# TensorE's order written out by hand in the attention stage: expert steps with attention pieces between them, and the first chunk's chain ahead of the second's

## The chip, the cores and the metric

The kernel runs on one core of one Trainium2 chip. The time is device microseconds for one execution of the whole program, the median of three runs. The engines are TensorE (PE; its weight loads are listed as PEld), VectorE (DVE), ScalarE (ACT), GpSimd (POOL) and SyncE (SP), which issues nearly all DMAs here. Each engine executes its instructions in the order in which they stand in the program.

## What is computed

Two parts, one behind the other. First a linear attention with complex, diagonal decay, over 4 batches, 8 heads, 768 positions and 48 dimensions; its output, as 3072 tokens of 384, is the input of a mixture of eight experts whose weights P are balanced over all tokens:

```python
# attention
scale = np.minimum(mag, 0.999) / (mag + 1e-06)      # mag = |a|
for t in range(S):
    S_re, S_im = ar * S_re - ai * S_im, ar * S_im + ai * S_re
    S_re = S_re + k[t] outer v[t]
    y[t] = q[t] @ S_re
# experts, x = y as (3072, 384)
P = np.exp(x @ w_gate - max)
for _ in range(8):
    P /= P.sum(1, keepdims=True) + 1e-09
    P /= P.sum(0, keepdims=True) + 1e-09
    P *= N / E
for e in range(E):                                   # w1: 384 x 1024, w2: 1024 x 384
    out += P[:, e:e + 1] * (np.maximum(x @ w1[e], 0.0) @ w2[e])
```

## The kernel before

The tokens are cut into 12 sub-chunks of 256, three for each batch, and each sub-chunk into two chunks of 128. Four kinds of work touch a sub-chunk i.

`elem(i)` (L262) is the elementwise part, on DVE and ACT. `chain` (L313) normalises the decays, forms their running products (a scan of complex products, `cmul`, L244 to 260), divides the keys by them (kh, L376) and multiplies the queries with them (z, L381). Both go to DRAM (kd, L377; qd, L382), since attention needs them with heads in another layout. For sub-chunk 0 the two chunks have a chain each; the later ones do both chunks in one.

`mix(i)` (L384) is the attention of the sub-chunk. It loads keys (ks, L397) and queries (qs, L398) back from DRAM into two buffers that the chunks use in turn; the last column of qs holds the chunk's total decay, which ACT copies into rr and rn (L400 to 402). For each chunk and each group of four heads PE transposes keys (ktp, L417; copied to kt on ACT, L419), forms the chunk's state contribution (U, L421) and the scores (sp, L424; DVE copies their lower triangle into sc, L427), and multiplies scores with values and queries with the state so far into the output (y, L438). Then DVE updates the state (L448 to 459). The output is x, split into a high and a low half (xh, L461; xl, L462) so that matmuls with the fast type keep float32 precision.

`logits(i)` (L466) makes the gate's logits of a sub-chunk. A `moe` step (L142) is 128 of one expert's 1024 hidden units for the 256 tokens: nine layer-1 matmuls (ph, L162 to 164), a relu that ACT writes twice (hh, L168; hf, L169), the difference on DVE (hl, L170), and six layer-2 matmuls (po, L152 to 154). Only experts 0 and 1 are computed in this way, 16 steps for each sub-chunk and 192 in all. Their weights are split into two halves by `load_w` (L124), with PE matmuls against the identity (wd, L136 and 137).

The program is written as mix(i), then the 16 steps of sub-chunk i-1, then elem(i+1), and a scheduler decides each engine's order in this part, from that order of writing and from a simulated timeline. The steps of the last two sub-chunks are written behind the first half of the balancing of P (check, L481; `sinkhorn`, L497; `rows` and `columns`, L514 to 528, of whose eight iterations four run here and where each column sum needs a PE matmul, L524). The last stage, experts 2 to 7 (from the first product P, L693), already has PE's order fixed by the order of writing.

Of the kernel before, what the change touches and what calls it, by code (L numbers as in the profile page):

```python
# [13 lines left out]
H, D = 8, 48  # L14
# [10 lines left out]
RING = 12  # L25
TR = 4
# [25 lines left out]
class Net:  # L52
# [9 lines left out]
    def build(self):  # L62
# [3 lines left out]
        with ExitStack() as ctx:  # L66
# [38 lines left out]
            with ExitStack() as c2:  # L105
                with ExitStack() as c1:
                    with ExitStack() as ca:
                        self.phase1(c1, ca)
                    self.phase2a(c2)
                    for u in range(2):  # L110
                        for i in range(ns - 2, ns):
                            self.moe1(i, (u,))
                        if u == 0:
                            self.raw_w()
                            self.prep_w()
                            self.prep_w()
                with tc.manual_schedule(engines={mybir.EngineType.PE}):
                    self.phase2b(c2)
# [5 lines left out]
    def load_w(self, e, f, pool, stage, tag):  # L124
        nc = self.nc
        t = pool.tile([128, 2, 2 * C], F32R, tag="w", name=f"w{e}_{f}")
        raw = stage.tile([128, 2 * C], F32, tag=tag, name=f"wr{e}_{f}")
        nc.sync.dma_start(raw, self.w[e, f])
        nc.scalar.activation(t[:, 0, :], raw, AF.Copy)
        for j in range(2):  # L130
            cs = slice(j * C, j * C + C)
            if j == 0:
                d = self.psA.tile([128, C], F32, tag="ph", name=f"wd{e}_{f}_{j}")
            else:
                d = self.psB.tile([128, C], F32, tag="po", name=f"wd{e}_{f}_{j}")
            nc.tensor.matmul(d, self.ident, raw[:, cs], start=True, stop=False)  # L136
            nc.tensor.matmul(d, self.nident, t[:, 0, cs], start=False, stop=True)
            nc.scalar.activation(t[:, 1, cs], d, AF.Copy)
        self.wt[e, f] = t

    def moe(self, e, fs, xs, T, done):
        nc = self.nc  # L142
        nt = T // 128
        po = [self.psB.tile([128, C], F32, tag="po", name=f"po{e}_{i}") for i in range(nt)]
        pend = []

        def l2(f, hh, hl, first, last):
            w2h = self.wt[e, f][:, 0, C:]
            w2l = self.wt[e, f][:, 1, C:]
            for i in range(nt):  # L150
                s = slice(i * 128, i * 128 + 128)
                nc.tensor.matmul(po[i], hh[:, s], w2h, start=first, stop=False)  # L152
                nc.tensor.matmul(po[i], hh[:, s], w2l, start=False, stop=False)  # L153
                nc.tensor.matmul(po[i], hl[:, s], w2h, start=False, stop=last)  # L154

        xh, xl = xs
        for j, f in enumerate(fs):
            w = self.wt[e, f]
            ph = self.psA.tile([128, T], F32, tag="ph", name=f"ph{e}_{f}")
# [5 lines left out]
            hh = self.hp.tile([128, T], F32R, tag="hh", name=f"hh{e}_{f}")  # L165
            hl = self.hp.tile([128, T], F32R, tag="hl", name=f"hl{e}_{f}")
            hf = self.hp.tile([128, T], F32, tag="hf", name=f"hf{e}_{f}", bufs=2)
# [3 lines left out]
            pend.append((f, hh, hl, j == 0, j == len(fs) - 1))  # L171
            if len(pend) > 1:
                l2(*pend.pop(0))
        l2(*pend.pop(0))
        for i in range(nt):
            done(i, po[i])

    def phase1(self, c1, ca):
# [31 lines left out]
        units = [(0, list(range(NF))), (1, list(range(N1)))]  # L210
        self.units = units
        self.elem(0, True)
        for f in range(NF):
            self.load_w(0, f, self.wp, wx, "w")
        for f in range(N1):
            if NF + f < RING:
                self.load_w(1, f, self.wp, wx, "w")
            else:
                self.load_w(1, f, wx, self.xp, "xh" if f % 2 else "xl")
        for i in range(ns):  # L220
            self.mix(i)
            if i == ns - 1:
                self.logits(i)
            if i > 0 and i + 1 < ns:
                self.moe1(i - 1)
            if i + 1 < ns:
                with ExitStack() as ctx:
                    if i == 0:
                        ctx.enter_context(tc.issue_after(self.gl.ins))
                    self.elem(i + 1)  # L230

    def moe1(self, i, us=(0, 1)):
        nc = self.nc
        for u in us:
            e, fs = self.units[u]

            def done(k, po, u=u, i=i):
                st = self.xp.tile([128, C], F32, tag="yst", name=f"yst{u}_{i}_{k}")
                nc.scalar.activation(st, po, AF.Copy)
                nc.sync.dma_start(self.ye_d[u][i * (SUB // 128) + k], st)  # L240

            self.moe(e, fs, self.xs[i], SUB, done)

    def cmul(self, L, R, n, alloc):  # L244
# [15 lines left out]
        V.tensor_tensor(R[:, 1], a[:, 1], b[:, 0], ALU.add)  # L260
# [51 lines left out]

    def chain(self, i, ns_, zt, qk, alloc):  # L313
# [25 lines left out]
        zr = z.rearrange("p a g (r b) -> p a g r b", r=TR)  # L339
        for r in range(1, TR):  # L340
            self.cmul(zr[:, :, :, r - 1], zr[:, :, :, r], TB, alloc)
        ze = zr[:, :, :, TR - 1]
        for r in range(1, TR):
            self.cmul(ze[:, :, :, r - 1::TR], ze[:, :, :, r::TR], TB // TR, alloc)
        d = 1
        while d < TB // TR:
            m = TB // TR - d
            self.cmul(ze[:, :, :, TR - 1:TR - 1 + TR * m:TR], ze[:, :, :, TR - 1 + TR * d::TR], m, alloc)
            d *= 2
        zs = ze.rearrange("p a g (c s) -> p a g c s", s=TR)  # L350
        m = TB // TR - 1
        sh = list(zs[:, :, :, 1:, :TR - 1].shape)
        self.cmul(zs[:, :, :, :m, TR - 1:].broadcast_to(sh), zs[:, :, :, 1:, :TR - 1], m * (TR - 1), alloc)
        for r in range(0, TR - 1, 2):
            R = zr[:, :, :, r:min(r + 2, TR - 1), 1:]
            L = ze[:, :, :, :TB - 1]
            if R.shape[3] == 1:
                self.cmul(L, zr[:, :, :, r, 1:], TB - 1, alloc)
            else:
                self.cmul(L.unsqueeze(3).broadcast_to(list(R.shape)), R, R.shape[3] * (TB - 1), alloc)  # L360
# [3 lines left out]
        nc.scalar.activation(sq, z, AF.Square)  # L364
# [10 lines left out]
        for a in range(2):  # L375
            V.tensor_tensor(kh[:, a], x, z[:, a], ALU.mult)  # L376
            nc.sync.dma_start(  # L377
                kd[a, :, ns_].rearrange("(c p) n t -> p c (n t)", c=NCT),
                kh[:, a].rearrange("p (c n) t -> p c (n t)", c=NCT))
        for a in range(2):  # L380
# [5 lines left out]
    def mix(self, i):  # L386
# [6 lines left out]
        for c in range(NCH):  # L393
# [15 lines left out]
            for g in range(2):  # L409
                hs = range(4 * g, 4 * g + 4)  # L410
                if not lastc:
                    if i == 0:
                        kt_p = self.psB.tile([128, 4, SK], F32, tag="po", name=f"ktp{i}_{c}_{g}")
                    else:
                        kt_p = self.psS.tile([128, 4, SK], F32, tag="s", name=f"ktp{i}_{c}_{g}")
                    for j, h in enumerate(hs):
                        nc.tensor.transpose(kt_p[:, j, :], ks[:, h, :], self.ident[:SK, :SK])  # L417
                    kt = tmp.tile([128, 4, SK], F32, tag="kt", name=f"kt{i}_{c}_{g}", bufs=2)
                    nc.scalar.activation(kt, kt_p, AF.Copy)  # L419
                    for j, h in enumerate(hs):  # L420
                        nc.tensor.matmul(U[:, h, :], kt[:, j, :], vt[:, c, slot(h):slot(h) + D], start=True, stop=True)  # L421
                sp = self.psS.tile([128, 4, CH], F32, tag="s", name=f"sp{i}_{c}_{g}")
                for j, h in enumerate(hs):
                    nc.tensor.matmul(sp[:, j, :], ks[:, h, :], qs[:, h, :CH], start=True, stop=True)  # L424
                ss = self.sc[self.isc]
                self.isc = 1 - self.isc
                nc.vector.copy_predicated(ss, self.mask, sp)  # L427
                for b in range(2):
                    for inter in range(1 if first else 2):
                        for j, h in enumerate(hs):  # L430
# [4 lines left out]
                            rw = qs[:, h, :CH] if inter else ss[:, j, :]  # L435
# [3 lines left out]
            if c == 0 and i > 0:  # L439
                self.logits(i - 1)  # L440
# [22 lines left out]
        for a, t in ((0, xh), (1, xl)):  # L463
            nc.sync.dma_start(self.x_d[i // NS][:, i % NS, a], t.bitcast(F32).rearrange("p c (j t) -> p c j t", t=CH))

    def logits(self, i):  # L466
# [7 lines left out]
        nc.scalar.activation(ls, lp, AF.Copy)  # L474
        lt = self.psS.tile([128, SUB // 128, E], F32, tag="s", name=f"lt{i}")
# [3 lines left out]
        nc.scalar.activation(self.P[:, i * n:(i + 1) * n, :], lt, AF.Copy)  # L479

    def check(self, sp):  # L481
# [9 lines left out]
        nc.vector.tensor_reduce(ok[:, 7:8], ok[:, 0:7], AX.X, ALU.min)  # L491
        tp = self.psK.tile([1, 128], F32, tag="po", name="okp")
# [4 lines left out]
    def sinkhorn(self, sp):  # L497
# [433 lines left out]
```

## Time and profile before

| | us |
|---|---|
| median of three runs | 1891.73 (1889.19 to 1897.45) |
| the profiled execution, own time | 1894.79 |
| its span in the profile | 1892.9 |
| PE busy in the span | 1794.9 (95%) |
| DVE busy | 1362.0 (72%) |
| ACT busy | 732.9 (39%) |
| first product P of the last stage | 717 |

The span is what the trace covers; the execution's own time has 1.9 us around it. The stages of the span are: start, with the weights of experts 0 and 1 and sub-chunk 0 (to 120 us); attention with the steps of sub-chunks 0 to 9 between (120 to about 652); the first half of the balancing with the last steps (652 to 717); experts 2 to 7 (717 to 1893).

### The profile page before, as it was taken

To read this page: it belongs to the slowest core of one execution; us is meant where nothing else is said; L and a number is where in the kernel's file an instruction comes from. 1 tells how busy PE (TensorE), PEld (TensorE's weight loads), DVE (VectorE), ACT (ScalarE), POOL (GpSimd) and SP (SyncE) were. 2 spreads that over 40 slices of the span, in tenths; PEclk is the share of its full clock that TensorE was granted. 3 is DMA by queue.
4 is the path that set the end of the run, shared out by engine and by line. 5 is a ranking of instruction groups with operands and counts; after the bars stand their busy time and mean duration, and the time that the engine had idled before them with its cause. 6 is when DMAs were issued, how large, how long until landed. Compare 5 with 4: busy or idle time off the path is not lost.

```text
span 1892.9 us, 30256 instructions
## 1 busy us (share of the span) xinstructions
PE 1794.9 (95%) x12012; PEld 1745.2 (92%) x12012; DVE 1362.0 (72%) x3060; ACT 732.9 (39%) x1610; POOL 6.4 (0%) x15
## 2 busy tenths in 40 slices
PE   5879988898999999999999999999999999999998
PEld 3779888888989999999999999999999999999998
DVE  7777778878877377876767676778786767676754
ACT  7434444444443353433333333334342424242421
POOL 1000000000000000000000000000000000000000
PEclk9888999999899999999999999999999999999999
DMA  6555555665454322220101010123130201010100
GB/s 199 128 136 120 145 146 138 146 146 128 136 127 117 118 92 68 84 84 17 51 17 51 18 51 17 51 92 125 51 101 1 67 1 57 11 51 17 51 22 31
DMA packets 137207, 151.84 MB, mean 80 GB/s; under 512 B 7264, under 2 KB 116576, under 8 KB 137056
## 3 DMA queue, kind: packets, MB, share of 16 engines
q1 hardware_dynamic: 136256, 149.42, 28.5%
q8 instruction: 96, 1.57, 0.3%
q14 instruction: 55, 0.45, 0.1%
q10 hardware_dynamic: 800, 0.39, 0.1%
HBM read 107.17 MB, written 42.61 MB: 79 GB/s over the span
## 4 chain that ended last, share of the span: by engine, by line
PE 73%; DMA 12%; DVE 10%; ACT 2%; issue 2%; SPq 1%; DVEq 0%; ACTq 0%
PE po L656 10%; PE po L654 10%; PE po L655 10%; PE P L693 9%; PE P L695 9%; PE P L694 9%; DMA qs<-qd 4%; DMA qd<-z 3%; PE po L152 2%; PE ph L162 2%; PE ph L163 2%; PE po L154 2%; PE po L153 2%; PE ph L164 2%; PE sp L424 2%
## 5 line engine op out<-in xcount | busy, mean ns | idle before, releaser
L656 PE MATMUL po<-wc,hl 128*128 128x384 f32 x1152 | 385.6, 335 | 1.9 <-DVE hl L715 1.8
L654 PE MATMUL po<-wc,hh 128*128 128x384 f32 x1152 | 385.2, 334 | 0.0
L655 PE MATMUL po<-wc,hh 128*128 128x384 f32 x1152 | 385.2, 334 | 0.0
L714 ACT ACTIVATE hh<-c 128x384 fp32r<-128x384 f32 x384 | 201.1, 524 | 319.5 <-DVE c L703 318.0
L715 DVE SCALAR_TENSOR_TENSOR hl<-c,hh 128x384 fp32r<-128x384 f32 x384 | 212.2, 553 | 66.6 <-ACT hh L714 58.6
L656 PEld LDWEIGHTS po<-wc,hl 128*128 128x128 f32 x1152 | 216.5, 188 | 2.9 <-DVE hl L715 2.9
L655 PEld LDWEIGHTS po<-wc,hh 128*128 128x128 f32 x1152 | 216.5, 188 | 0.0
L654 PEld LDWEIGHTS po<-wc,hh 128*128 128x128 f32 x1152 | 216.5, 188 | 0.0
L708 ACT ACTIVATE s<-P 128x384 f32<-128x384 f32 x192 | 94.2, 491 | 276.7 <-PE P L695 276.4
L162 PE MATMUL ph<-xh,w 128*128 128x256 f32 x576 | 166.2, 289 | 7.7 <-ACT hf L169 5.8
L163 PE MATMUL ph<-xl,w 128*128 128x256 f32 x576 | 166.2, 289 | 4.8 <-DVE xl L462 4.8
L164 PE MATMUL ph<-xh,w 128*128 128x256 f32 x576 | 165.3, 287 | 0.0
L693 PE MATMUL P<-B,wa 128*128 128x384 f32 x480 | 160.7, 335 | 1.4 <-DVE c L703 1.4
L695 PE MATMUL P<-B,wa 128*128 128x384 f32 x480 | 160.5, 334 | 0.0
L694 PE MATMUL P<-B,wa 128*128 128x384 f32 x480 | 160.5, 334 | 0.0
L170 DVE TENSOR_TENSOR hl<-hf,hh 128x256 fp32r<-128x256 f32 x192 | 79.5, 419 | 100.1 <-ACT hf L169 96.6
L152 PE MATMUL po<-w,hh 128*128 128x384 f32 x384 | 137.0, 357 | 1.3 <-ACT hh L168 1.3
L153 PE MATMUL po<-w,hh 128*128 128x384 f32 x384 | 132.0, 344 | 0.0
L703 DVE TENSOR_TENSOR c<-P,u 128x384 f32<-128x384 f32 x192 | 106.4, 554 | 31.4 <-PE P L695 29.8
L168 ACT ACTIVATE hh<-ph 128x256 fp32r<-128x256 f32 x192 | 73.0, 380 | 142.5 <-PE ph L164 135.8
L703 DVE TENSOR_TENSOR u<-u,s 128x384 f32<-128x384 f32 x96 | 53.4, 556 | 100.2 <-ACT s L708 99.9
L162 PEld LDWEIGHTS ph<-xh,w 128*128 128x128 f32 x576 | 111.7, 194 | 9.4 <-ACT hf L169 6.3
(182 smaller groups left out, 3686.0 us busy)
## 6 DMA issues: line engine op xcount, KB each, us to landing
raw<-in_w_dram SPq DMA_DIRECT2D x48, 768.0 KB, 4.3
qs<-qd SPq DMA_DIRECT2D x48, 193.5 KB, 7.8
qk<-in_aqk_dram SPq DMA_DIRECT2D x12, 768.0 KB, 9.3
ks<-kd SPq DMA_DIRECT2D x48, 192.0 KB, 6.1
ye_d<-yst SPq DMA_DIRECT2D x48, 192.0 KB, 2.2
y<-ye_d SPq DMA_DIRECT2D x48, 192.0 KB, 2.4
qd<-z SPq DMA_DIRECT2D x22, 390.0 KB, 6.2
z<-in_aqk_dram SPq DMA_DIRECT2D x11, 768.0 KB, 10.3
```

The lines of the kernel that those rows point to most:

```text
L152: nc.tensor.matmul(po[i], hh[:, s], w2h, start=first, stop=False)
L162: nc.tensor.matmul(ph, w[:, 0, cs], xh[:, ct, :], start=(ct == 0), stop=False)
L163: nc.tensor.matmul(ph, w[:, 0, cs], xl[:, ct, :], start=False, stop=False)
L164: nc.tensor.matmul(ph, w[:, 1, cs], xh[:, ct, :], start=False, stop=(ct == NCT - 1))
L654: nc.tensor.matmul(po[k], hh[:, s], w2[:, 0, i], start=first, stop=False)
L655: nc.tensor.matmul(po[k], hh[:, s], w2[:, 1, i], start=False, stop=False)
L656: nc.tensor.matmul(po[k], hl[:, s], w2[:, 0, i], start=False, stop=last)
L693: nc.tensor.matmul(ps, t[:, 0, k], x[:, 0], start=first, stop=False)
L694: nc.tensor.matmul(ps, t[:, 0, k], x[:, 1], start=False, stop=False)
L695: nc.tensor.matmul(ps, t[:, 1, k], x[:, 0], start=False, stop=last)
L714: A.activation(hh, c, AF.Relu)
L715: V.scalar_tensor_tensor(hl, c, 0.0, hh.bitcast(F32), ALU.max, ALU.subtract)
```

## The change

PE's order is now the order of writing in the whole program, and that order is written out by a loop:

- A generator `experts()` issues steps one after another over all experts and sub-chunks, with layer 2 two steps behind layer 1 (LAG = 2) where it was one behind.
- `mix(i)` is a generator of ten pieces, five for each chunk: keys and scores of head group 0; state of group 0 and keys of group 1; outputs of group 0 and scores of group 1; state of group 1; outputs of group 1 and the end of the chunk.
- In period i (1 to 11) the 16 steps of sub-chunk i-1 are issued as n = 0 to 15, and behind each from n = 4 (LEAD) on one piece of mix(i), so pieces stand at n = 4 to 13. Logits of i-1 stand behind n = 1 and 2.
- Expert 1's weights f = 4 to 7 come late, in eight halves behind steps n = 0 to 7 of period 1 (`load_late`); f = 0 to 3 come between pieces of mix(0), behind chunk 0's keys.
- Behind the last attention output only sub-chunk 11's steps remain: two with its logits, then 14 at fixed places in the balancing (`more`). The first weights of the last stage are prepared after the second iteration.
- In sub-chunk 0 chunk 1's scan is issued behind the end of chunk 0's.

DVE, ACT and SP still get their order from the scheduler. The core of the diff:

```diff
+LAG = 2
+LEAD = 4
-            with ExitStack() as c2:
+            with ExitStack() as c2, tc.manual_schedule(engines={mybir.EngineType.PE}):
...
-                    for u in range(2):
-                        for i in range(ns - 2, ns):
-                            self.moe1(i, (u,))
-                with tc.manual_schedule(engines={mybir.EngineType.PE}):
-                    self.phase2b(c2)
+                self.phase2b(c2)
...
+    def load_late(self, e, f, j, wx):
+        raw = self.xp.tile([128, C], F32, tag="yst", name=f"wr{e}_{f}_{j}")
+        nc.sync.dma_start(raw, self.w[e, f, :, cs])
+        nc.scalar.activation(t[:, 0, cs], raw, AF.Copy)
+        d = self.psS.tile([128, C], F32, tag="s", name=f"wd{e}_{f}_{j}")
+        nc.tensor.matmul(d, self.ident, raw, start=True, stop=False)
+        nc.tensor.matmul(d, self.nident, t[:, 0, cs], start=False, stop=True)
+        nc.scalar.activation(t[:, 1, cs], d, AF.Copy)
...
+            if len(pend) == LAG:
+                l2(*pend.pop(0))
...
         for i in range(ns):
-            self.mix(i)
-            if i == ns - 1:
-                self.logits(i)
-            if i > 0 and i + 1 < ns:
-                self.moe1(i - 1)
+            mix = self.mix(i)
+            if i == 0:
+                for n, _ in enumerate(mix):
+                    if n % 2 == 0 and n < 2 * (RING - NF):
+                        with tc.issue_after(self.kd0.ins), tc.issue_after(self.sq0.ins):
+                            self.load_w(1, n // 2, wx)
+                with tc.issue_after(self.gl.ins):
+                    self.elem(1)
+                continue
+            lg = self.logits(i - 1)
+            for n in range(2 * NF):
+                self.moe.send((i - 1, n // NF, n % NF))
+                if n in (1, 2):
+                    next(lg)
+                if late:
+                    self.load_late(*late.pop(0), wx)
+                if n >= LEAD:
+                    next(mix, None)
...
+        if full or n0 == 0:
+            self.scan(z, alloc)
+        else:
+            with self.tc.issue_after(self.last.ins):
+                self.scan(z, alloc)
...
+            keys(0)
+            scores(0)
+            yield
+            state(0)
+            keys(1)
+            yield
+            outs(0)
+            scores(1)
+            yield
+            state(1)
+            yield
+            outs(1)
...
         for k in range(ITERS // 2):
             self.rows()
+            more(2)
             self.columns(self.psK.tile([128, E], F32, tag="po", name=f"cp{k}"))
+            if k == 1:
+                self.raw_w()
+                self.prep_w()
+                self.prep_w()
+        more(len(todo))
```

Three places of the new order. A row is line, operation, written tile, read tiles and shape; xN stands for N such rows in a run.

PE, where mix(1) begins. Before, its first scores (sp_0_0) stand behind layer 2 of expert 1's step 6 and 7 (hh_6, hh_7; the weights w_6 and w_7 are expert 1's), so behind all 16 steps of sub-chunk 0:

```order
L421 MATMUL U_0_853<-v_724,kt_0_0_859 112x48 x4
L154 MATMUL po_0_1212<-w_6_544,hl_6_1351 128x384
L154 MATMUL po_1_1213<-w_6_544,hl_6_1351 128x384
L152 MATMUL po_0_1212<-w_7_556,hh_7_1372 128x384
L153 MATMUL po_0_1212<-w_7_556,hh_7_1372 128x384
L152 MATMUL po_1_1213<-w_7_556,hh_7_1372 128x384
L153 MATMUL po_1_1213<-w_7_556,hh_7_1372 128x384
L424 MATMUL sp_0_0_865<-qs_173,ks_175 128x128 x4
```

Now they stand behind layer 1 of expert 0's step 4 (ph_0_4: sub-chunk 0, step 4), with a late half of expert 1's weights (wd_6_0) between:

```order
L178 MATMUL ph_0_4_924<-xh_474,w_4_426 128x256
L140 MATMUL wd_6_0_944<-wr_6_0_941,ident 128x384
L141 MATMUL wd_6_0_944<-w_6_940,nident 128x384
L438 MATMUL ktp_0_0_959<-ident,ks_177 128x112 x4
L452 MATMUL sp_0_0_966<-qs_175,ks_177 128x128 x4
L155 MATMUL po_0_0_853<-w_3_414,hh_0_3_905 128x384
L156 MATMUL po_0_0_853<-w_3_414,hh_0_3_905 128x384
```

Five steps stand ahead of mix(1) where there were 16.

DVE, around the end of sub-chunk 0's chains. Before, both chunks' key products (kh_208) and query products (z_197) are done ahead of sub-chunk 1's scan (cm_a, cm_b into z_722), which has begun where the masked copy of the first scores (sc_177) stands:

```order
L376 TENSOR_TENSOR kh_208<-x_209,z_197 128x3x128 x2
L332 TENSOR_TENSOR x_731<-x_731,zz_733 128x768
L381 TENSOR_TENSOR z_197<-z_197,qk_198 128x3x128 x2
L333 SCALAR_TENSOR_TENSOR y_732<-x_731,y_732 128x768
L335 TENSOR_SCALAR x_731<-y_732 128x768
L336 SCALAR_TENSOR_TENSOR x_731<-zz_733,x_731 128x768
L338 TENSOR_TENSOR z_722<-z_722,x_731 128x6x128 x2
L255 TENSOR_TENSOR cm_a<-z_722 128x12x32
L255 TENSOR_TENSOR cm_b<-z_722 128x12x32
```

Now chunk 1's key products (kh_210) and query products (z_199) stand behind the masked copy of chunk 0's first scores (sp_0_0), which the rows here begin with:

```order
L455 COPY_PREDICATED sc_179<-mask,sp_0_0_492 128x512
L387 TENSOR_TENSOR x_211<-x_211,zz_213 128x384
L388 SCALAR_TENSOR_TENSOR zz_213<-x_211,zz_213 128x384
L363 SCALAR_TENSOR_TENSOR x_685<-sq_684 128x768
L389 SCALAR_TENSOR_TENSOR x_211<-zz_213,qk_200 128x384
L393 TENSOR_TENSOR kh_210<-x_211,z_199 128x3x128 x2
L400 TENSOR_TENSOR z_199<-z_199,qk_200 128x3x128 x2
L455 COPY_PREDICATED sc_180<-mask,sp_0_1_529 128x512
```

A little further on, sub-chunk 1's scan (cm_a, cm_b into z_676) begins behind the masked copy of chunk 1's first scores (sp_1_0):

```order
L370 SCALAR_TENSOR_TENSOR x_685<-zz_687,x_685 128x768
L372 TENSOR_TENSOR z_676<-z_676,x_685 128x6x128 x2
L455 COPY_PREDICATED sc_179<-mask,sp_1_0_594 128x512
L265 TENSOR_TENSOR cm_a<-z_676 128x12x32
L265 TENSOR_TENSOR cm_b<-z_676 128x12x32
```

Two copies of scores, each behind a load from DRAM, have moved ahead of work that the next load needs.

ACT, in the middle of the stage. Before, the four copies rr (of both query buffers, qs_173 and qs_174) stand together between two sub-chunks' steps (hh_7 is the last step of one, hh_0 the first of the next):

```order
L168 ACTIVATE hh_7_3992<-ph_7_3982 128x256
L169 ACTIVATE hf_7_3994<-ph_7_3982 128x256
L419 ACTIVATE kt_0_0_4153<-ktp_0_0_4148 128x448
L400 ACTIVATE rr_189<-qs_173 48x8
L401 ACTIVATE rr_189<-qs_173 48x8
L400 ACTIVATE rr_190<-qs_174 48x8
L401 ACTIVATE rr_190<-qs_174 48x8
L168 ACTIVATE hh_0_4316<-ph_0_4306 128x256
```

Now the copies of the second buffer (qs_176), which hold the next sub-chunk's chunk 1, stand between the last two steps of a sub-chunk (hh_5_6, hh_5_7):

```order
L182 ACTIVATE hh_5_6_4640<-ph_5_6_4630 128x256
L183 ACTIVATE hf_5_6_4642<-ph_5_6_4630 128x256
L379 ACTIVATE z_5342<-z_5342 128x12 x2
L419 ACTIVATE rr_192<-qs_176 48x8
L420 ACTIVATE rr_192<-qs_176 48x8
L182 ACTIVATE hh_5_7_4662<-ph_5_7_4652 128x256
L183 ACTIVATE hf_5_7_4664<-ph_5_7_4652 128x256
L421 ACTIVATE rn_194<-qs_176 48x8
```

The copies of the first buffer moved too; they stand earlier in the sub-chunk's second eight steps, on their own.

More of the change, by code (lines that the diff above doesn't have):

```diff
@@ L148, in l2, with experts @@
+    def experts(self):
+        nc = self.nc
+        pend, po = [], {}
+        def l2(i, e, f, hh, hl):
             w2h = self.wt[e, f][:, 0, C:]
             w2l = self.wt[e, f][:, 1, C:]
[L150 to L154, printed above, removed]
@@ L232, in moe1 @@
[L232 to L242, printed above, removed]
+            self.load_w(0, f, wx)
+        late = [(1, f, j) for f in range(RING - NF, NF) for j in range(2)]
@@ L244, in cmul @@
+        lg = self.logits(ns - 1)
+        for f in range(2):
+            self.moe.send((ns - 1, 0, f))
+            next(lg)
     def cmul(self, L, R, n, alloc):
@@ L408, in mix @@
             U = self.psY.tile([SK, H, D], F32, tag="U", name=f"U{i}_{c}")
[L409 to L421, printed above, removed]
+            kts, sss = {}, {}
@@ L425, in mix, with outs @@
-                ss = self.sc[self.isc]
+                for j in range(4):
+                    nc.tensor.matmul(sp[:, j, :], ks[:, 4 * g + j, :], qs[:, 4 * g + j, :CH], start=True, stop=True)
+                ss = sss[g] = self.sc[self.isc]
                 self.isc = 1 - self.isc
                 nc.vector.copy_predicated(ss, self.mask, sp)
+            def outs(g, c=c, xp=xp, qs=qs, sss=sss, S0=S0, first=first):
                 for b in range(2):
                     for inter in range(1 if first else 2):
-                        for j, h in enumerate(hs):
+                        for j in range(4):
+                            h = 4 * g + j
@@ L501, in sinkhorn @@
         mp = self.psK.tile([1, 128], F32, tag="po", name="mp")
+        more(1)
         nc.tensor.transpose(mp, mx, self.ident)
```

178 lines of the change are left out of this document (101 added, 77 removed).

## The prediction

> **What bounds the kernel now.** I read the span by stages first, then what TensorE (PE) waits for in the attention stage, then single rows. Stage table: start and end, length, then busy us of PE, weight load, DVE, ACT and GpSimd, granted PE clock, DMA share, GB/s.
>
> ```profile
> 0.00:120.00 120.00, 86.26 (x525) 70.17 (x526) 86.73 (x261) 64.31 (x146) 6.36 (x15) 0.90 0.66 171
> 120.00:610.00 490.00, 446.95 (x4024) 424.39 (x4023) 394.42 (x924) 209.85 (x546) 0.00 (x0) 0.94 0.53 130
> 652.00:717.00 65.00, 64.03 (x451) 63.06 (x450) 44.57 (x132) 33.24 (x87) 0.00 (x0) 1.00 0.36 112
> 717.00:1893.00 1176.00, 1156.70 (x6633) 1149.64 (x6631) 822.04 (x1710) 411.55 (x789) 0.00 (x0) 1.00 0.15 48
> ```
>
> PE is the bound; behind the start no other engine is busy for more than 81% of a stage. From 652 us on PE is full, at full clock. In the attention stage, 120 to 610 us, it idles 490 - 447 = 43 us, and the missing clock, 6% of 490, costs 29 us more. These 72 us are all that a better order can win there. What PE waits for in that stage (total us, times, longest):
>
> ```profile
> PE sp L424 <- DMA qs<-qd: 15.4, 5, 5.9
> PE ktp L417 <- DMA ks<-kd: 6.1, 3, 3.2
> PE ph L163 <- DVE xl L462: 4.5, 3, 2.2
> PE po L154 <- DVE hl L170: 2.4, 2, 1.6
> PE y L438 <- DVE sc L427: 1.7, 3, 0.8
> ```
>
> The two largest are loads of queries and keys: PE reached an attention matmul before its data was back from DRAM.
>
> The last stage, from the first product P (L693) at 717 us, is not touched and keeps its 1176 us. So I forecast when that P starts.
>
> **What PE's pieces cost.** One stretch of the timeline: start, length, engine, line, names, shapes. A length includes the pipeline, so I take distances between starts.
>
> ```profile
> 593.09 0.61 PE L477 MATMUL lt<-two,ls 16*128 16x8 f32 x4
> 593.63 0.60 PE L417 MATMUL ktp<-ident,ks 112*128 112x112 f32 x4
> ...
> 594.67 0.34 PE L152 MATMUL po<-w,hh 128*128 128x384 f32 x1
> 594.84 0.33 PE L153 MATMUL po<-w,hh 128*128 128x384 f32 x1
> 595.02 0.28 PE L162 MATMUL ph<-xh,w 128*128 128x256 f32 x1
> 595.13 0.28 PE L163 MATMUL ph<-xl,w 128*128 128x256 f32 x1
> ...
> 596.43 1.06 PE L424 MATMUL sp<-qs,ks 112*128 112x128 f32 x8
> 597.33 0.90 PE L421 MATMUL U<-v,kt 128*112 128x48 f32 x8
> 598.06 0.57 PE L417 MATMUL ktp<-ident,ks 112*128 112x112 f32 x4
> 598.40 0.42 PE L152 MATMUL po<-w,hh 128*128 128x384 f32 x1
> ...
> 602.72 0.43 PE L438 MATMUL y<-sc,v 128*32 128x128 f32 x8
> 602.96 0.40 PE L438 MATMUL y<-qs,st 112*32 112x128 f32 x8
> ```
>
> An expert step is nine layer-1 matmuls at about 0.12 and six layer-2 matmuls at about 0.174: 1.08 + 1.04, some 2.15 us. A head group of attention is 0.90 (sp) + 0.73 (U) + 0.34 (ktp) + 4 x 0.23 (y) = 2.9; four make 11.5, and logits add 6 x 0.12 + 0.54 = 1.3. A batch's last chunk has no ktp and U (2.1 less, three of the eleven later sub-chunks), so a sub-chunk averages 12.2 and eleven are 134 us.
>
> **The change, term by term.**
>
> *Start.* Before, DVE runs both chunks' chains together:
>
> ```profile
> 44.60 1.02 DVE L376 TENSOR_TENSOR kh<-x,z 128x384 f32<-128x384 f32 x2
> 46.40 1.02 DVE L381 TENSOR_TENSOR z<-z,qk 128x384 f32<-128x384 f32 x2
> 53.00 0.56 DVE L255 TENSOR_TENSOR cm_a<-z 128x384 f32<-128x384 f32 x1
> 58.95 0.21 ACT L402 ACTIVATE rn<-qs 48x8 f32<-48x8 f32 x1
> 100.95 0.96 DVE L381 TENSOR_TENSOR z<-z,qk 128x768 f32<-128x768 f32 x1
> 119.69 1.13 PE L424 MATMUL sp<-qs,ks 112*128 112x128 f32 x8 [2.12 <-DMA qs<-qd]
> 53.00:102.00 49.00, 43.34 (x362) 40.12 (x361) 36.88 (x90) 22.77 (x57) 0.00 (x0) 0.89 0.48 116
> ```
>
> From chunk 1's last z (47.4) to its queries on the chip (58.95) are 11.5 us. After, chunk 0's keys come, as an estimate, 9 us sooner, since its scan no longer shares DVE, and its scores run near 49. But the masked copy of those scores now stands on DVE ahead of chunk 1's key and query products, and the copy of chunk 1's scores ahead of sub-chunk 1's whole scan; both wait for data on its way through DRAM. So chunk 1's z ends near 57, its queries land near 69, and sub-chunk 1's scan starts near 71 instead of 53.0. Before, that scan and its products took 53.0 to 101.9, but DVE worked only 36.9 of those 49 us; after, with most waits already behind it, I allow 38. Its z then ends near 109, and with the 17.8 us from z to first scores as before (101.9 to 119.69) mix(1) begins near **127**, 7 us later than before. Bounds: 119.7 if DVE's waits are covered, 138 if all 18 us of delay pass through. And ahead of mix(1) PE may now do only five steps (LEAD is 4) where 16 stood before; it will idle some 30 us there, and eleven steps, 24 us, move behind.
>
> *Work from there.* 192 steps less 5 are 187 x 2.15 = **402**; eleven sub-chunks **134**; three of the late weight halves, 0.82 each by the distance of two such pairs, **2.5** (the other five fall into the idle start). Their eight loads on SP and sixteen copies on ACT run beside that idle start and the first steps; expert 1's first four tiles, now held behind chunk 0's keys, are only needed eight steps later. I cost both at nothing; without that cover a late half would cost a step's wait, 2.15 us, inside the bounds of the start.
>
> ```profile
> 20.63 0.81 PE L136 MATMUL wd<-wr,ident 128*128 128x384 f32 x2
> ...
> 21.45 0.81 PE L136 MATMUL wd<-wr,ident 128*128 128x384 f32 x2
> ```
>
> *End.* Before, 30 steps lay behind the last attention output and PE was full, Sinkhorn hidden. After, 18 are left (38.7 us), and its column sums stand at fixed places between them. The chain that they wait for:
>
> ```profile
> 650.88 0.40 PE L438 MATMUL y<-qs,st 112*32 112x128 f32 x8
> 679.41 0.52 DVE L520 TENSOR_REDUCE cs<-P 128x8 f32<-128x192 f32 x1
> 681.93 0.29 PE L524 MATMUL cp<-cs,ones 128*128 128x8 f32 x2
> 687.22 0.51 DVE L520 TENSOR_REDUCE cs<-P 128x8 f32<-128x192 f32 x1
> ```
>
> First column sum 29 us behind the last output, then 5.8 per iteration: 29 + 3 x 5.8 = 46.4, so **8** us of PE waiting. Bounds: 0, if less other DVE work shortens the chain, and 15. The first expert weights of the last stage are now prepared after the second iteration; the two iterations that remain, 11.6 us, cover it, and late by a whole one (5.8) it still lies inside these bounds.
>
> *Stops in the periods.* Waits for queries and keys should go: the order holds each piece back, DVE runs a sub-chunk ahead. What is late next is ACT. It executes in order, and the copy rr of the next sub-chunk's chunk-1 queries now stands ahead of hh of the period's last step. That load can start only when outs(1) has freed its buffer, two steps before the end. Rows (ACT waits; the page's issue-to-landing time; the split's lengths):
>
> ```profile
> ACT rr L400 <- DMA qs<-qd: 49.2, 16, 7.5
> qs<-qd SPq DMA_DIRECT2D x48, 193.5 KB, 7.8
> L170 DVE TENSOR_TENSOR hl<-hf,hh 128x256 fp32r<-128x256 f32 x192 | 79.5, 419 | 100.1 <-ACT hf L169 96.6
> L168 ACT ACTIVATE hh<-ph 128x256 fp32r<-128x256 f32 x192 | 73.0, 380 | 142.5 <-PE ph L164 135.8
> ```
>
> Landing 7.8, two rr 0.42, hh and hf 0.76, hl 0.42: 9.4 us, against three steps, 6.45, before PE needs that hl: up to 3 us per period. Nine periods at 3 are 27; at 0, when two loads instead of four share the queues, nothing. I take 2: **18**. The other three rows of PE's waits (4.5 + 2.4 + 1.7 = 8.6) I keep, less a little for layer 2's second step of distance: **8**.
>
> Sum: 127 + 402 + 134 + 2.5 + 8 + 18 + 8 = 699.5, against 717: 17.5 us won. Span 1892.9 - 17.5 = 1875.4; the profiled run's own 1894.79 becomes 1877.3; it lay 3 us above the median of the runs, 1891.7, so the time is **1874**.
>
> One row speaks against a long stop. PE is busy 2.84 of the 5 us from 105, and in the next 5 its clock is 0.66, a loss of 1.7 us:
>
> ```profile
> 105.00:110.00 5.00, 2.84 (x21) 2.58 (x19) 4.46 (x11) 1.32 (x4) 0.00 (x0) 1.00 1.13 285
> 110.00:115.00 5.00, 4.22 (x20) 4.25 (x21) 0.59 (x2) 1.05 (x3) 0.00 (x0) 0.66 1.07 214
> ```
>
> The Trainium skill ("TensorE: Matmul & The Clock Gate", "What's actually happening") says that an idle window of about 3.4 us halves PE's clock until about 3.4 us of sustained work have passed. The two rows agree with it; by that rule each stop of 3.4 us or more costs about 1.7 us on top, and the restart case below would follow from it.
>
> **Rivals.** (1) *Dense:* queries land in time, DVE's start is covered: rr 0, end 4, others 2, start 122: 717 - 666.5 = 50 won, 1842. For it: qs pairs are now issued apart. Against: ACT's rr waits of 3.1 us mean (49.2 / 16) stand in the trace already. (2) *A wash:* the chunk-1 rr stop is whole, ten times 3.1 = 31 instead of 18, 712.5: 1887. (3) *Slower:* the rr of both chunks stop ACT and with it PE, which had slack because the scheduler let layer 2 or attention run in any place, and a fixed order has not: ten periods x 2 x 3.1 = 62 instead of 18, 743.5: 1918. It decides from stops of 3.6 us a period (18 + 17.5 over ten). (4) *Restart:* the chunk-1 stop is whole (31) and each of the ten is followed by the clock loss of the row at 110 us, 1.7: 699.5 + 13 + 17 = 729.5, so 1904. Against it: 3.1 us is shorter than the idle time around 108. (5) *The order is not what holds PE:* the idle moves from queries to DVE, which is busy 394 of 490 us and in order too, and nothing changes: 1892.
>
> **How the numbers follow.** My case 0.45, dense 0.12, wash 0.14, slower 0.17, restart 0.05, nothing 0.07. My case runs from 1856 (rr 0) to 1883 (rr 27). The start (119.7 to 138) and rr (0 to 62) are open, so the range reaches from near the dense case to near the slower one: 1846 to 1912. About 9.5 us, 0.5%, can be told from no change: faster 0.57 (my case, dense), same 0.21 (wash, nothing), slower 0.22 (slower, restart).
>
> **What would show it.** First scores of sub-chunk 1 at 120 to 138 us, with PE idle for 25 to 35 us before. No wait of sp or ktp on qs or ks from period 2 on; a wait of layer 2 (hl) once per period behind ACT's rr, 0 to 3 us. Granted clock in the attention stage above 0.94. First P at about 700, the 1176 us behind it unchanged. I am wrong if waits on hl or masked scores appear in most steps (fixed order too tight), or if first P comes later than 717.

## The result, and the profile after

The changed kernel takes 1901.41 us (median of 14 runs, 1899.28 to 1904.32), the kernel before 1890.43 us on the same chips. The ratio is 1.0058, 95% interval 1.0048 to 1.0069: slower by about 11 us, where 17.5 us of gain were forecast. The profiled execution has a span of 1902.5 us.

The stages of the changed kernel: start and end, length, busy us of PE, weight load, DVE, ACT and GpSimd, then granted clock, DMA share, GB/s:

```profile
0.00:120.00 120.00, 59.08 (x340) 44.30 (x340) 86.32 (x248) 55.30 (x119) 6.36 (x15) 0.78 0.55 148
120.00:610.00 490.00, 458.88 (x4123) 432.76 (x4123) 394.13 (x932) 219.75 (x577) 0.00 (x0) 0.98 0.49 134
610.00:680.00 70.00, 68.98 (x650) 65.66 (x646) 24.22 (x60) 23.42 (x68) 0.00 (x0) 1.00 0.30 92
680.00:730.00 50.00, 44.40 (x294) 42.22 (x295) 40.12 (x120) 26.53 (x65) 0.00 (x0) 1.00 0.43 136
```

PE does 27 us less in the first 120 us, as forecast, and in the attention stage its idle time falls from 43 to 31 us and the clock's loss from 29 to 10. So the order did win there, but less than it cost at the start. Only five steps now stand ahead of the first scores of sub-chunk 1 instead of sixteen, about 24 us of work at 2.15 us a step, and these scores come at 127.24 us instead of 119.69: some 31 us lost. From them to the first P the new order takes 599.0 us with that work added, where the old one took 595.8, by this row of the kernel before: some 20 us won.

```profile
715.53 0.33 PE L693 MATMUL P<-B,wa 128*128 128x384 f32 x1
```

What PE waits for from 120 to 610 us now (total us, times, longest):

```profile
PE po L157 <- DVE hl L184: 11.3, 15, 2.1
PE po L155 <- ACT hh L182: 10.8, 6, 4.1
PE sp L452 <- DMA qs<-qd: 7.9, 1, 7.9
```

The waits for keys and queries are gone but for one, the start of mix(1). In their place layer 2 waits for its own inputs: for hh, which ACT makes (10.8 us), and for hl, which DVE makes from ACT's hf (11.3 us, 2.4 before). ACT itself waits in the stretch from 100 to 700 us like this:

```profile
ACT rr L419 <- DMA qs<-qd: 63.4, 19, 8.1
ACT rn L421 <- DMA qs<-qd: 17.8, 15, 4.4
```

Three moments place the loss. First scores of sub-chunk 1, the last attention output, and the first P:

```profile
127.24 2.05 PE L452 MATMUL sp<-qs,ks 112*128 112x128 f32 x8 [7.90 <-DMA qs<-qd]
...
674.52 0.40 PE L469 MATMUL y<-qs,st 112*32 112x128 f32 x8
...
726.22 0.33 PE L757 MATMUL P<-B,wa 128*128 128x384 f32 x1
```

The start was forecast at 127 and is at 127.24. From there to the first P are 599.0 us, where the forecast's sum had 572.5: all of the miss, 26.5 us, lies in the periods and the end. What happens there is seen in period 2. DVE and SP first, then ACT:

```profile
207.76 0.95 DVE L400 TENSOR_TENSOR z<-z,qk 128x768 f32<-128x768 f32 x1
208.96 0.95 DVE L400 TENSOR_TENSOR z<-z,qk 128x768 f32<-128x768 f32 x1
...
208.73 0.36 SPq L401 DMA_DIRECT2D qd<-z  x1
209.94 0.41 SPq L401 DMA_DIRECT2D qd<-z  x1
212.54 0.31 SPq L417 DMA_DIRECT2D qs<-qd  x1
215.49 0.30 SPq L417 DMA_DIRECT2D qs<-qd  x1
...
215.51 0.38 ACT L183 ACTIVATE hf<-ph 128x256 f32<-128x256 f32 x1
221.76 0.21 ACT L419 ACTIVATE rr<-qs 48x8 f32<-48x8 f32 x1 [5.87 <-DMA qs<-qd]
221.88 0.47 ACT L503 ACTIVATE xh<-y 128x384 fp32r<-128x384 f32 x1
222.37 0.21 ACT L420 ACTIVATE rr<-qs 48x8 f32<-48x8 f32 x1
224.25 0.21 ACT L421 ACTIVATE rn<-qs 48x8 f32<-48x8 f32 x1 [1.66 <-DMA qs<-qd]
224.36 0.36 ACT L182 ACTIVATE hh<-ph 128x256 fp32r<-128x256 f32 x1
```

DVE finishes the two halves of the next sub-chunk's queries at 208.7 and 209.9. They go to DRAM and come back, each with its own write (qd) and load (qs). ACT's rr reads the first half and can run at 221.76, 13 us after it was made; rn reads the second and can run at 224.25, 14 us after. Between the relu that ends at 215.9 and the one at 224.36 ACT does none. On PE, layer 1 of the next step ends, and layer 2 stands:

```profile
220.37 0.28 PE L178 MATMUL ph<-xh,w 128*128 128x256 f32 x1
224.78 0.69 PE L155 MATMUL po<-w,hh 128*128 128x384 f32 x1 [4.13 <-ACT hh L182]
```

This is chunk 0's copy, ahead of the relus of the last two steps; in later periods it stands further forward. Chunk 1's, on which the forecast had put its price, follows at 229.58. And the data was late because DVE had only just made it, not because a buffer was still in use: SP issued the load at 212.54, as soon as the write of 208.73 had landed. From 100 to 640 us its loads of queries wait for such a write 13 times, 23.0 us in all, and for readers of the buffer (y and sb) six times, 12.6 us.

### The profile page after: what moved, and what is told of

It is laid out like the page before. It is cut to its first block, busy times and chain, and to the rows that moved or that the text cites. A ratio compares the mean times of both kernels' runs of the same rounds, so it can differ in the third digit from the quotient of the medians.

```text
span 1902.5 us, 30283 instructions
## 1 busy us (share of the span) xinstructions
PE 1784.5 (94%) x12012; PEld 1730.6 (91%) x12012; DVE 1364.5 (72%) x3060; ACT 735.3 (39%) x1614; POOL 6.4 (0%) x15
## 4 chain that ended last, share of the span: by engine, by line
PE 75%; DVE 11%; DMA 9%; ACT 3%; issue 2%; SPq 1%; DVEq 0%; ACTq 0%
PE po L720 10%; PE po L719 10%; PE po L718 10%; PE P L757 9%; PE P L758 9%; PE P L759 9%; DMA qs<-qd 4%; PE po L157 2%; PE po L155 2%; PE ph L177 2%; PE ph L178 2%; PE ph L176 2%; PE po L156 2%; PE sp L452 2%; DMA qd<-z 1%
## 5 line engine op out<-in xcount | busy, mean ns | idle before, releaser
L176 PE MATMUL ph<-xh,w 128*128 128x256 f32 x576 | 163.2, 283 | 0.6 <-ACT xh L503 0.6
L178 PE MATMUL ph<-xh,w 128*128 128x256 f32 x576 | 163.3, 283 | 0.0
L155 PE MATMUL po<-w,hh 128*128 128x384 f32 x384 | 142.5, 371 | 11.4 <-ACT hh L182 11.2
L157 PE MATMUL po<-w,hl 128*128 128x384 f32 x384 | 134.2, 349 | 13.7 <-DVE hl L184 12.5
L156 PE MATMUL po<-w,hh 128*128 128x384 f32 x384 | 130.5, 340 | 0.0
```

What stands on the lines that cost most here:

```text
L155: nc.tensor.matmul(po[k], hh[:, s], w2h, start=f == 0, stop=False)
L176: nc.tensor.matmul(ph, w[:, 0, cs], xh[:, ct, :], start=(ct == 0), stop=False)
L178: nc.tensor.matmul(ph, w[:, 1, cs], xh[:, ct, :], start=False, stop=(ct == NCT - 1))
```

## The experiments

Times are medians; the ratio is to the kernel before on the same chip, with its 95% interval. "The changed kernel" is 1901.4 us. Runs on other chips are set against it by their medians, while the kernel before differed by up to 3 us from chip to chip (1890.4 to 1893.4); so differences of a few us are no more than hints.

### Both decay copies later

```diff
-            nc.scalar.activation(rr[0:D], R[0:D], AF.Copy)
-            nc.scalar.activation(rr[64:64 + D], R[0:D], AF.Copy)
-            nc.scalar.activation(rn[0:D], R[64:64 + D], AF.Copy, scale=-1.0)
...
             yield
+            with ExitStack() as ctx:
+                if i:
+                    ctx.enter_context(tc.issue_after(self.hf.ins))
+                nc.scalar.activation(rr[0:D], R[0:D], AF.Copy)
+                nc.scalar.activation(rr[64:64 + D], R[0:D], AF.Copy)
+                nc.scalar.activation(rn[0:D], R[64:64 + D], AF.Copy, scale=-1.0)
             outs(1)
```

`self.hf` is the hf relu of the latest step, which the edit keeps for this.

> The changed kernel, with ACT's decay copies rr and rn of each chunk moved behind the hf of the step at which the chunk's last outputs stand, so that no relu waits behind a load of queries. Theory A (ACT's order costs the periods): from the first scores of sub-chunk 1 at 127 us to the last attention output at 675 us PE loses 48 us against its work, most of it because hh and hl of one or two steps per period are held behind rr; then ACT's waits of rr for qs fall from 63 us to under 10, the last output comes 15 to 30 us sooner, and the time falls from 1901 to about 1880. Theory B (the fixed order itself is too tight: hl waits its turn on DVE, rr only looks like the cause): the waits of layer 2 for hl and hh stay at 20 us or more and the time falls by less than 6.

1870.79 us, ratio 0.9882 (0.9850 to 0.9914): 30.6 us under the changed kernel (33 by the ratios), above what theory A asked for. ACT's list of waits from 100 to 700 us has no wait of rr or rn for qs left. The attention stage, and PE's waits in it:

```profile
120.00:610.00 490.00, 480.10 (x4409) 461.13 (x4410) 403.28 (x946) 230.46 (x609) 0.00 (x0) 0.99 0.51 140
...
PE sp L449 <- DMA qs<-qd: 8.1, 1, 8.1
PE po L157 <- DVE hl L184: 2.7, 3, 1.7
```

PE now idles 10 us in that stage, 8 of them in the one wait at its start, and waits for hh are gone. The last attention output comes at 640.39 instead of 674.52, with the first scores at 125.85: 514.5 us for the same work instead of 547.3, with every matmul on PE in the same order as before the edit. Theory B falls by its own sign; the fixed order is not too tight by itself, with layer 2 two steps behind.

One thing more changed with the edit. DVE's order is still the scheduler's, and it put hl nearer behind hf: between 130 and 640 us hl begins 0.62 us behind the end of its hf in the mean, where it was 1.06 in the changed kernel. There, most of PE's waits for hl ended on an hl that began 2 to 4 us behind its hf, because products of the scan stood ahead of it on DVE:

```profile
431.51 0.38 ACT L183 ACTIVATE hf<-ph 128x256 f32<-128x256 f32 x1
433.99 0.42 DVE L184 TENSOR_TENSOR hl<-hf,hh 128x256 fp32r<-128x256 f32 x1
434.46 0.44 PE L157 MATMUL po<-w,hl 128*128 128x384 f32 x1 [0.95 <-DVE hl L184]
```

So the place of the copies is the cause of the 31 us; how much of it is ACT's stops themselves and how much the order that DVE got along with them, no run separates.

### Chunk 1's copies alone

The same edit under `if c == 1:`, chunk 0's copies left where they were.

> The changed kernel with only chunk 1's copies rr and rn moved behind the step's hf; chunk 0's stay where the scheduler put them. The prediction's picture (chunk 1's rr, ahead of the last step's hh, is what stops PE; chunk 0's is covered): most of the 30 us that moving both copies won, 1876 or lower. Theory A0 (chunk 0's carries more: in the changed kernel's trace ACT waits 4 to 8 us for it in periods 2 to 7, for chunk 1's 0 to 5): 5 to 12 us won, 1890 to 1896.

1897.62 us, ratio 1.0028 (1.0013 to 1.0044): 3.8 us of the 30.6 by the medians, 5.7 of 33 by the ratios. The prediction's picture falls; A0's range is met at its low end at best. ACT still waits 39.8 us for chunk 0's rr, and the wait at the start of mix(1) is as it was. So most of the loss goes only when chunk 0's copies move too. Whether they would do it alone was not tried.

### Layer 2 three steps behind

```diff
-LAG = 2
+LAG = 3
-        self.hp = c1.enter_context(tc.tile_pool(name="hp1", bufs=3))
+        self.hp = c1.enter_context(tc.tile_pool(name="hp1", bufs=4))
```

> The changed kernel with layer 2 three steps behind layer 1 instead of two (and a fourth buffer for hh and hl). Theory A: a stop of up to 3 us behind rr is covered by one more step of 2.15 us, so most of PE's 24 us of named waits for hh and hl goes, time 10 to 20 lower, near 1886. Theory B (DVE has too little time in a period, whatever the distance): the waits return a step later, under 6 us gained.

1889.28 us, ratio 0.9990 (0.9972 to 1.0008): 12 us under the changed kernel, theory A's range. The distance covers part of each stop. ACT's rr waits stay (75.1 us), and PE waits earlier in the step instead:

```profile
PE ph L176 <- ACT hf L183: 11.5, 8, 2.7
```

Layer 1 needs one of the two PSUM buffers for ph, and hf has not read it yet. So one step more hides 12 us, and the removal of the cause wins 31.

### The second scan free again

```diff
-        if full or n0 == 0:
-            self.scan(z, alloc)
-        else:
-            with self.tc.issue_after(self.last.ins):
-                self.scan(z, alloc)
+        self.scan(z, alloc)
```

> The changed kernel without the rule that chunk 1's scan is issued behind chunk 0's. Theory C (the start pays for it): sub-chunk 1's scan no longer waits on DVE behind masked copies of scores; first scores of sub-chunk 1 at about 120 us instead of 127, time 7 lower, near 1894. Rival: the earlier first scores (48 us) save as much elsewhere, and nothing changes or it gets slower by up to 5.

1885.72 us, ratio 0.9975 (0.9958 to 0.9993): 15.7 us under the changed kernel, twice what theory C expected. With the rule, DVE (in the changed kernel) stands still until chunk 1's scores are there, and only then begins sub-chunk 1's scan; without it, that scan is begun before the first scores. Changed kernel first, then this run:

```profile
70.83 0.73 DVE L455 COPY_PREDICATED sc<-mask,sp 128x512 f32<-128x512 uint8 x1 [6.01 <-PE sp L452]
71.46 0.54 DVE L265 TENSOR_TENSOR cm_a<-z 128x384 f32<-128x384 f32 x1
...
110.28 1.82 DVE L400 TENSOR_TENSOR z<-z,qk 128x768 f32<-128x768 f32 x2
```

```profile
47.02 0.56 DVE L265 TENSOR_TENSOR cm_a<-z 128x384 f32<-128x384 f32 x1
...
54.38 0.73 DVE L451 COPY_PREDICATED sc<-mask,sp 128x512 f32<-128x512 uint8 x1 [5.66 <-PE sp L448]
...
107.49 2.05 PE L448 MATMUL sp<-qs,ks 112*128 112x128 f32 x8 [10.81 <-DMA qs<-qd]
```

First scores of sub-chunk 1 stand at 107.5, 20 us before the changed kernel's and 12 before the kernel before's (119.7). So the rest of the change makes the start better, and this one rule takes more than that away.

### Both edits together

> Both copies moved, and without the rule that chunk 1's scan is issued behind chunk 0's. If the two costs are separate (30.6 and 15.7 us, one in the periods and one in the start) they add: 1855. Rival: an earlier start only shifts waiting to DVE's chain of sub-chunks, and no more than 6 is won over moving the copies alone: 1865 or above.

1854.46 us, ratio 0.9806 (0.9780 to 0.9832). The two costs add: 1901.4 - 30.6 - 15.7 = 1855.1. That the sum is met within a microsecond is luck, since the interval alone is 10 us wide; that they are separate is not, since the rival asked for 1865 or more. Together they are 47 us, more than four times the change's net loss.

### Thirteen steps ahead of mix(1)

```diff
-                if n >= LEAD:
+                if n >= (12 if i == 1 else LEAD):
```

> The changed kernel with LEAD 12 instead of 4 in period 1 alone: 13 steps of sub-chunk 0 ahead of mix(1) instead of 5, and its last six pieces without steps between. Theory D (PE's idle 27 us ahead of mix(1) are lost for good): eight steps, 17 us, go into that idle time, some 6 us come back as stops between the six bare pieces: time 8 to 17 lower, near 1890. Rival: what sets the end is DVE's chain of sub-chunk after sub-chunk, and PE's steps only fill; then under 3 us.

1905.74 us, ratio 1.0073 (1.0047 to 1.0100): nothing won; the 4 us more are not clear of noise, since the intervals overlap. Theory D falls, though the steps do run in the idle time: logits of sub-chunk 1, behind the third step of period 2, come 12.5 us earlier (168.07 against 180.55). To see what takes it back, the same with both copies moved:

> Both copies moved (the rule on chunk 1's scan kept), and LEAD 12 in period 1. LEAD 12 by itself won nothing: the 12 us ahead at the first logits were gone by period 3. If ACT's rr stops took them back, they stay now: 8 to 12 us under the run with both copies moved, near 1860. If DVE's chain took them back (sub-chunk 2's queries are not there when the earlier steps run out), nothing stays: 1867 to 1874, with a wait of sp for qs in period 2.

1872.67 us, ratio 0.9894 (0.9877 to 0.9910), against 1870.79 without LEAD 12: DVE takes it back. The trace shows where: in period 2 PE is ahead of the data, waits for sub-chunk 2's queries, and runs at a lower clock around it.

```profile
180.82 2.05 PE L449 MATMUL sp<-qs,ks 112*128 112x128 f32 x8 [7.11 <-DMA qs<-qd]
...
160.00:200.00 40.00, 32.66 (x258) 31.31 (x257) 29.61 (x76) 13.20 (x35) 0.00 (x0) 0.81 0.63 139
```

DVE's key products of sub-chunk 2 also begin later, at 159.57 instead of 152.46 for the run with the copies alone; the hl of eight more steps stand ahead of them on DVE. The stops between the bare pieces of mix(1), which the expectation put at 6 us, came as well: 3.1 and 0.5 us for masked scores and 2.6 for xl. The idle time ahead of mix(1) is thus DVE's chain seen from PE. Filling it with steps wins nothing; making that chain start earlier does.

### Six more steps beside the balancing

With both edits, mix(11)'s pieces stand behind steps 0 to 9 of period 11, and the last six steps of sub-chunk 10 move behind the last output.

```diff
+            lead, steps = (0, 10) if i == ns - 1 else (LEAD, 2 * NF)
-            for n in range(2 * NF):
+            for n in range(steps):
...
-                if n >= LEAD:
+                if n >= lead:
...
-        todo = [(n, e, f) for e in range(2) for f in range(NF)][2:]
+        todo = [(i, e, f) for i in (n - 1, n) for e in range(2) for f in range(NF)][10 + 2:]
```

> As the run with both edits, and in period 11 the pieces of mix(11) stand behind steps 0 to 9, so that the last attention output comes six steps earlier and 24 steps instead of 18 lie beside the balancing. Theory E (PE idles 12 to 15 us there because 18 steps, 38.7 us, are shorter than the chain of column sums): 8 to 13 us lower than the run with both edits, near 1845. Rival: mix(11)'s keys are not there that early, and the gain comes back as a wait for ks or qs; then under 3 us.

1847.39 us, ratio 0.9766 (0.9747 to 0.9785): 7.1 us under both edits, a microsecond short of theory E's range. In the changed kernel PE waited behind steps for the column sums, 4.4 us in all, and the run with both edits does the same; here it does so less (first the changed kernel's rows, then this run's wait):

```profile
706.38 0.39 PE L573 MATMUL cp<-cs,ones 128*128 128x8 f32 x2 [1.41 <-DVE cs L569]
712.10 0.39 PE L573 MATMUL cp<-cs,ones 128*128 128x8 f32 x2 [0.98 <-DVE cs L569]
...
723.77 0.39 PE L573 MATMUL cp<-cs,ones 128*128 128x8 f32 x2 [2.02 <-DVE cs L569]
```

```profile
PE cp L573 <- DVE cs L569: 2.0, 4, 1.2
```

But that is less than half of the gain. The first P comes 3.2 us earlier than with both edits (672.70 against 675.87), and the other 4.3 us are won behind it, where nothing was edited: there the run with both edits has stretches at half clock that this run does not have. With both edits, then here (length, busy us of PE, granted clock, DMA share, GB/s):

```profile
670.00:680.00 10.00, 7.98 (x40) 0.83 0.35 119
680.00:690.00 10.00, 8.12 (x39) 0.87 0.70 198
```

```profile
670.00:680.00 10.00, 9.48 (x53) 1.00 0.50 160
680.00:690.00 10.00, 8.32 (x48) 1.00 0.56 158
```

The missing clock, 0.17 and 0.13 of 10 us each, is some 3 us of the 4.3.

This is the fastest kernel of the study: 43 us under the kernel before, 54 under the changed one. With LEAD 8 in period 1 as well:

> The fastest run so far (copies moved, no rule on chunk 1's scan, earlier pieces in period 11) with LEAD 8 in period 1: four more steps, 8.6 us, in PE's idle time ahead of mix(1), two bare pieces. If that idle time is worth filling: 4 to 8 us lower, 1840 to 1843. If DVE's chain takes it back: within 2 of 1847.

1848.44 us, ratio 0.9774 (0.9756 to 0.9792), the same within the intervals, as the run with LEAD 12 had shown already.

### The decay copies in the kernel before

```diff
-            nc.scalar.activation(rr[0:D], R[0:D], AF.Copy)
...
             if not lastc:
+                with self.tc.issue_after(last.ins):        # the chunk's second kt
+                    nc.scalar.activation(rr[0:D], R[0:D], AF.Copy)
...
```

> The kernel before (the scheduler's order on PE), with rr and rn issued behind the chunk's second key copy kt (and left out in a batch's last chunk, where nothing reads them). If PE had other work in its order while ACT waited, as the prediction said of before, ACT's 49 us of rr waits were mostly covered: 0 to 6 us lower, 1885 to 1891. Rival: the rr waits held PE up before the change too, and the gain of moving them has little to do with the fixed order: 15 us or more lower.

1881.20 us, ratio 0.9942 (0.9924 to 0.9960): 11 us won, between the two expectations. That suggests that the scheduler's order was not free of this cost and paid about a third of what the fixed order pays (11 against 30.6). It does not show it: here the scheduler wrote PE a new order too, and the copies stand at another place, so the 11 us are the copies and the new order together. With the copies out of the way in both, the changed kernel is 1881.2 - 1870.8 = 10 us faster than the kernel before with the rule on chunk 1's scan, and 1881.2 - 1854.5 = 27 us without it; that is the worth of the rest of the change as a whole.

## Why the prediction was wrong

*What bounds the kernel; the untouched last stage.* Right: the first P comes at 726.22, and 1176.3 us follow. In the kernel before, the first P stands at 715.53, not 717, so 1177.4 us followed it there.

*Start, 127 us.* Right in its mechanism: DVE's scan of sub-chunk 1 was forecast at 71 and begins at 71.46, and the first scores come at 127.24. That the figure is met so closely is partly luck. Its z ends at 112.1 against 109, and from z to first scores it takes 15.1 us instead of 17.8: the two misses cancel. And the 11.5 us from chunk 1's z to its queries were misread. The copy at 58.95 is of chunk 0's queries; chunk 1's load was issued only at 55.47, and the copy that waits for it is at 66.85, in the kernel before:

```profile
55.47 1.28 SPq L398 DMA_DIRECT2D qs<-qd  x2
66.85 0.21 ACT L402 ACTIVATE rn<-qs 48x8 f32<-48x8 f32 x1 [1.13 <-DMA qs<-qd]
```

That way took 19.4 us there, and takes 13.0 in the changed kernel (55.74 to 68.69). Right too was that the masked copies ahead of it are the reason; the run without the rule shows it. What I had wrong is what would be without them: not the old 119.7 but 107.5, so the rule's price is 20 us in this moment and 15.7 in the time, not 7.

*Eleven steps that move behind the start, 24 us.* The sum counts them rightly, but they were no choice of the order: with the steps put ahead, PE waits for the next sub-chunk's queries instead.

*Stops in the periods, 18 us.* This is the step that failed, and it is the one that turned a gain into a loss. The prediction put them on chunk 1's rr, with its buffer's release as the last condition and a cover of three steps, and held that DVE runs a sub-chunk ahead, so that chunk 0's queries are there in time. The runs show 30.6 us in time, and 32.7 us less from first scores to last output when both copies are moved; moving chunk 1's alone gives 3.8. DVE is not far enough ahead: its queries are finished within the period, and then comes the way through DRAM, 13 to 14 us in period 2. The prediction had put 11.5 us on that way at the start and did not use it here. The case with both chunks' copies stood among the rivals with 62 us and a chance of 0.17; the mechanism is that one, at half its price.

*Others, 8 us, and the periods' work.* From first scores to last output the run without rr stops takes 514.5 us, where the sum's terms without rr give 402 + 134 + 2.5 + 8 less the 18 steps behind the last output (38.7): 507.8. So the sum is 6.7 us too low. It is not the waits: that run's waits of PE for other engines are 4.0 us in this stretch, not 8. About 2.5 us are the half clock from the first scores to 130.9. The rest, some 8 us as an estimate, is time that steps and pieces take beyond the 2.15 and 12.2 us they were priced at; the trace doesn't settle why.

*End, 8 us of waiting.* The 18 steps and the chain were forecast at 46.7 us; in the changed kernel it is 51.7 (674.52 to 726.22), 5 us more. But PE waits only 5.8 us in it, 4.4 of them for column sums. What the sum left out is work: layer 2 of two earlier steps also falls behind the last output (layer 2 of 20 steps and layer 1 of 18 stand there, 2.1 us more), and so do the logits of sub-chunk 11 (1.3 us) and the small matmuls of the balancing. The run with six more steps there wins 7.1 us, by fewer waits and by the clock behind them.

The three add up: 14.7 us on the rr stops (32.7 for 18), 6.7 and 5.0, with 0.2 at the start, make the 26.7 us between 726.2 and 699.5.

*Restart.* Present but small: the clock is 0.98 in the stage, so 10 us against 29 before. The row that the prediction set against this case was misread: PE's idle time around 108 us was 2.94 us (107.84 to 110.78), so shorter than both the 3.1 and the 3.4 us that the prediction holds against it, and the clock fell to half behind it all the same.

## What to carry to other kernels

When one engine's order is fixed by hand, an engine that feeds it can hold it up with an instruction that it does not need at that point: look on the feeding engines for every instruction that waits for a DMA and has matmul inputs queued behind it, and issue it where its data must already be there. A wait's price is counted from the moment its data is produced, with the whole round trip, not from the release of the buffer it lands in. And filling an idle stretch ahead of the first use of some data won nothing here, since it delayed the producer of the next data; letting the producer start earlier won 15.7 us.

## What the runs showed of the hardware

After the stop of 4.13 us at 220 us PE ran at half speed for 6.0 us, from 224.78 to 230.79: layer-2 matmuls 0.32 us apart instead of 0.174, layer-1 0.21 instead of 0.12. The windows around it (length, busy us of PE, granted clock, DMA share, GB/s):

```profile
220.00:225.00 5.00, 0.87 (x7) 0.90 1.20 236
225.00:230.00 5.00, 5.00 (x19) 0.50 0.94 272
```

So this stop costs about 3 us more than its own length (half of 6.0), where the prediction had counted 1.7. Other stops cost less. Behind one of 3.32 us that ends at 171.40, the matmuls run at half speed from 172.77 to 176.24, 3.5 us. Behind two short ones close together in the last stage, of 0.65 us up to 734.13 and of 1.08 us up to 736.00, they do so from 736.00 to 739.37, 3.4 us:

```profile
736.00 0.69 PE L720 MATMUL po<-wc,hl 128*128 128x384 f32 x1 [1.08 <-DVE hl L779]
...
735.00:740.00 5.00, 4.00 (x14) 0.66 0.57 158
```

The Trainium skill ("TensorE: Matmul & The Clock Gate", "What's actually happening") has the full clock back after at least one busy window of about 3.4 us; this trace shows it back 6.0, 4.8 and 3.4 us after the end of the three stops, and the measurement decides.

The length of a single stop does not settle whether the clock falls. Stops of up to 2.1 us, of which the later periods have many, leave it at 1.00 from 300 to 610 us. A stop of 2.02 us ahead of the last column sum leaves it at full in the changed kernel (up to 723.77), and is followed by half speed until 677.1 in the run with both edits (up to 672.50).
